# An early branch hint for TensorE's last block of instructions in a decode attention kernel

## Chip, cores, metric

The kernel runs on one core of a Trainium2 chip. The metric is the device time of one execution in microseconds (us), lower is better.

## What is computed

The reference is one decode step of grouped-query attention beside an MLP. Batch 2, one new token, model width 512, 32 query heads, 8 key/value heads, a cache of 32768 positions with head width 128, all in bfloat16. Cut to what matters:

```python
xn = layernorm(A_x)
q  = (xn @ A_wq).reshape(B, 1, 32, 128)
scores = einsum(q, repeat(k_cache, 4)) * 128 ** -0.5
o  = einsum(softmax(scores), repeat(v_cache, 4))
s  = o.reshape(B, 1, 32 * 128) @ A_wo
g  = silu(mlp_block(xn))      # with one position only w3, w4 matter
return A_x + s * g
```

The caches are 268 MB of the 280.5 MB that are read; wq, wo, w3 and w4 are the rest. With one position per sequence, the shifted halves of the MLP block are all padding, so the products with w1 and w2 contribute nothing and the kernel does not compute them.

## The kernel before

The work is cut into 16 groups, one for each pair of batch and key/value head. A group's keys are one transfer of 8 MB and its values another; the last group's are cut in halves. Both are written into fixed buffers (`kbuf`, three half-group slots that rotate; `vbuf`, two). All engines are synchronized by hand with semaphores inside one critical section: every engine has its own written order, wrapped by the small class `Queue` (waits, the instruction, an increment).

- The sync engine (SP) holds the queue of transfers: wq, w3, w4 and the first keys at the start (L310 to L313), then values and keys in turn as TensorE and ScalarE release the buffers (L448, L464, L469, L452), then wo in six parts (L477, L479; `wo_parts`, L240).
- VectorE transposes keys out of `kbuf` (L589), takes maxima, transposes the exponentials; it loops eight times over two groups each, with a branch hint of its own (L388 and L618).
- TensorE's program is written late: the prologue's products (x with wq, w3, w4) are collected in a `LateQueue` and placed at once (L685). It then waits for some constants (L686, L687), branches to the label `pe_groups` (L688), and loops 16 times over the body of one group (L689 to L734): 64 products for the scores (L698), the previous group's output (L660, L666), 64 products with the values (L722), some filling products (L673), and the closing compare-and-branch (L734). `turn` is the register that counts.
- Behind the loop stands `pe_output` (L737): the last group's output (L738 to L745), then the products on wo, part by part as they land (L746 to L773): parts for k below 5 at L760, the others at L768, between them the sum over the first (L750, which needs ScalarE's copy L646). VectorE multiplies and adds (L647, L648), and two small transfers write the result (L651).

A label with its body is a block of its own in the program; `nc.br` ends one block with a branch. The order of the instructions in memory is the order in which the blocks are written.

Of the kernel before, what the change touches and what calls it, by code (L numbers as in the profile page):

```python
# [13 lines left out]
PE = mybir.EngineType.PE  # L14
# [104 lines left out]
def kernel(  # L119
# [14 lines left out]
    nc = tc.nc  # L134
# [116 lines left out]
    def place(n):  # L251
        return n % OQ, slice(OJ - 1 - n // OQ, OJ - 1 - n // OQ + OM)

    def o_row(k, r):
        return oX[:, 1 + k:2 + k + (B - 1) * Hkv:Hkv, r]
# [47 lines left out]


    n_out = 16 * OQ
    nc.scalar.sem_inc(t_shift, n_out)
    with tc.tile_critical(sync_engine=mybir.EngineType.Pool, no_gpsimd_drain=True):
        nc.scalar.wait_ge(t_shift, n_out).then_inc(t_shift, -n_out)
# [28 lines left out]
        e_s00 = ve.op(lambda e: e.memset(sc[1][:, :], 0.0))  # L337
# [19 lines left out]
        with nc.allow_low_precision(reason="one of the terms is one, the others are zero"):  # L357
# [24 lines left out]
        e_const = ve.op(lambda v: v.tensor_copy(  # L382
            out=sel_w[:, :, :], in_=row_of[:, :].unsqueeze(1).broadcast_to([128, 4, 32])), e_row, e_ones)
# [15 lines left out]
        for i in range(NPART):  # L399
            for k in range(DK):  # L400
                for n in range(NQ):
# [5 lines left out]
                        e_xT, e_s00, inc=last)  # L407
# [13 lines left out]
        for k in range(DK):  # L421
# [7 lines left out]
        e_hf = ve.op(lambda v: v.tensor_copy(  # L429
            out=hf[:, :].rearrange("p (f b) -> p f b", b=B), in_=h4[:, :].rearrange("p (f c) -> p f c", c=32)[:, :, 0:B]), e)  # L430
# [11 lines left out]
        e_tf = ve.op(lambda v: v.tensor_add(out=t_f[:, :], in0=xn[:, :], in1=h2[0:B, :]), e_h2)  # L442
# [16 lines left out]
        e_s0 = ve.op(lambda v: v.memset(pro[:, :], 0.0))  # L459
# [21 lines left out]
        def take(eng, s, n=1):  # L481
            eng.wait_ge(s, n).then_inc(s, -n)  # L482
# [174 lines left out]
        def head_oT():  # L657
            take(nc.tensor, t_ob)
            for t in range(VT):
                ins = nc.tensor.matmul(  # L660
                    oT[:, :], lhsT=ob[:, t * Dh:(t + 1) * Dh], rhs=sel_o[:, t, :],
                    start=(t == 0), stop=(t == VT - 1))
            ins.then_inc(t_tv, 1)

        def head_xp():
            nc.tensor.matmul(  # L666
                xp_b[:, :], lhsT=sel_w[:, :, :].rearrange("p j w -> p (j w)"), rhs=on[:, :, :].rearrange("p r h -> p (r h)"),
                start=True, stop=True).then_inc(t_tv, 1)


        def fill(n):
            for _ in range(n):
                nc.tensor.matmul(pro[0:B, :], lhsT=comb[:, 0:B], rhs=ob[:, :], start=True, stop=True)  # L673

        def warm(n):
            for _ in range(n):
                nc.tensor.matmul(
                    sc[0][0:B, :], lhsT=pt[0][:, 0, 0:B], rhs=vbuf[:, 0:4 * Dh], start=True, stop=True)

        prologue, pe = pe, Queue(nc.tensor, pe.sem)  # L680
        pe.n, pe.seen = prologue.n + NG, prologue.seen
        assert prologue.n == pe_0
        turn = nc.alloc_registers("turn", engines=[PE])
        nc.regs_mov(turn, 0)
        prologue.place()  # L685
        for s, v in prologue._new((e_s00, e_const, e_hf, e_tf, e_s0)):  # L686
            nc.tensor.wait_ge(s, v)  # L687
        nc.br("pe_groups", engines=[PE])  # L688
        with nc.body("pe_groups", valid_engines=[PE]):  # L689
            for i in range(NPART):  # L690
                for r in range(NR):
# [45 lines left out]
        with nc.body("pe_output", valid_engines=[PE]):  # L737
            head_oT()  # L738
            pe.wait(e_sp, e_oX[NG - 2])
            pe.op(lambda t: t.matmul(  # L740
                wide, lhsT=sel_w[:, :, :].rearrange("p j w -> p (j w)"), rhs=oX_sp[:, :, :, :, :].rearrange("p k b j r -> p (k b j r)"),
                start=True, stop=True))
            fill(1)
            take(nc.tensor, t_vt)
            head_xp()  # L745
            for i, (a, c, r0, r1) in enumerate(wo_parts):  # L746
                if i == 3:
                    for n in range(NQ):
                        q, cols = place(n)
                        pe.op(lambda t, n=n, q=q, cols=cols: t.matmul(  # L750
                            pro[32 * q:32 * q + OM, 0:QW], lhsT=comb[:, cols], rhs=wsum[:, n * QW:(n + 1) * QW],
                            start=False, stop=False, tile_position=(0, 32 * q)), e_wsum, inc=False)
                for k in range(a, c):
                    pe.wait(e_oXz if k >= KC else e_oX[(B - 1) * Hkv + k], (d_wo[i], n_wo[i]), *((e_wide,) if i == 0 else ()))
                    for r in range(r0, r1):
                        gr = k * NQ + r
                        last = (i, k, r) == (len(wo_parts) - 1, c - 1, r1 - 1)
                        if k < KC:
                            lhs = oX_w.rearrange("p (b r) -> p b r", b=B)[:, :, gr] if i == 0 else o_row(k, r)
                            pe.op(lambda t, k=k, r=r, lhs=lhs: t.matmul(  # L760
                                qrb[32 * r:32 * r + B, :], lhsT=lhs, rhs=wo3[:, k, r * D:(r + 1) * D],
                                start=(k == 0), stop=(k == KC - 1), tile_position=(0, 32 * r)),
                                inc=(k == KC - 1 and r == NQ - 1))
                            continue
                        for n in range(NQ):
                            col = r * D + n * QW
                            q, cols = place(n)
                            pe.op(lambda t, k=k, r=r, n=n, q=q, cols=cols, col=col, last=last: t.matmul(  # L768
                                pro[32 * q:32 * q + OM, 0:QW], lhsT=oXz[:, k - KC, r, cols], rhs=wo3[:, k, col:col + QW],
                                start=(i == 2 and r == r0 and n < OQ), stop=(last and n >= NQ - OQ), tile_position=(0, 32 * q)),  # L770
                                inc=(last and n == NQ - 1))
                    if i == 2:
                        warm(1)  # L773
            nc.br("pe_done", engines=[PE])
# [37 lines left out]
```

## Time and profile before

| | |
|---|---|
| median of 3 runs | 656.04 us (655.86 to 656.45) |
| profiled execution: span, first to last instruction | 654.1 us |
| difference, what lies around the span and between executions | 1.94 us |
| PE / DVE / ACT busy | 64% / 58% / 6% |
| data queue (q1) | 280.50 MB, 99.2% of 16 DMA engines' span |
| instruction queue (q8) | 2 packets, 0.03 MB |
| mean granted TensorE clock | 0.880 |

How to read it: busy is the share of the span in which an engine executes; the DMA share is the mean over the core's 16 DMA engines, so one engine alone at work reads 0.06. Each stretch in the view by stretches has its length, the busy time of PE, PEld (weight loads), DVE, ACT and POOL with the number of instructions in brackets, the granted clock, the DMA share and GB/s. Line numbers (L698) are those of the kernel before. PEq, PEldq and DVEq rows are instructions of an engine's sequencer (branches, waits, moves).

### The profile page before, as it was taken

Reading aid. Unit: us, or ns where it says so; the run is one execution under the profiler, and the core shown is the slowest. Engines: PE = TensorE matmul, PEld = TensorE weight load, DVE = VectorE, ACT = ScalarE, POOL = GpSimd, SP = SyncE. Lnnn points to the kernel's source line nnn. Section 1 sums busy time; section 2 is a strip of 40 time slices with the busy share of each in tenths; the row PEclk is TensorE's granted clock in tenths of the full one; section 3 lists DMA queues with packets and bytes.
Section 4 is the critical chain, followed back from the end, with each engine's and each line's share of the span. In section 5 each row is a group of like instructions: output and inputs, shape, how many; then the busy total and the mean of one; then the engine's idle time right before and its main releaser. Section 6 shows DMA issues by size and latency. Waiting matters only on the chain. (4 is left out here: it accounts for less than half of the span.)

```text
span 654.1 us, 6304 instructions
## 1 busy us (share of the span) xinstructions
PE 417.4 (64%) x2476; PEld 159.3 (24%) x2476; DVE 379.4 (58%) x541; ACT 39.7 (6%) x90; POOL 10.3 (2%) x44
## 2 busy tenths in 40 slices
PE   1437386574858747485774838667484865748876
PEld 0013132221313212131321313222131322213223
DVE  5348193673919457291854729276481936738772
ACT  1200101000010100001000010100001010000101
POOL 1000000000000000000000000000000000000000
PEclk9859889697997969899796989969698896979999
DMA  8999999999999999998999999999999899999997
GB/s 367 435 449 449 442 393 449 445 449 401 437 445 449 433 405 449 445 449 389 449 445 449 417 421 445 449 445 393 449 445 449 389 449 445 449 425 411 437 429 292
DMA packets 6246, 280.54 MB, mean 429 GB/s; under 512 B 730, under 2 KB 868, under 8 KB 1380
## 3 DMA queue, kind: packets, MB, share of 16 engines
q1 hardware_dynamic: 6232, 280.50, 99.2%
q8 instruction: 2, 0.03, 0.0%
q10 hardware_dynamic: 12, 0.00, 0.0%
HBM read 280.50 MB, written 0.00 MB: 429 GB/s over the span
## 5 line engine op out<-in xcount | busy, mean ns | idle before, releaser
L589 DVE STREAM_TRANSPOSE T<-kbuf 128x1024 int32<-128x1024 int32 x256 | 294.8, 1211 | 180.1 <-DMA kbuf<-in_A_k_cache_dram 173.2
L698 PE MATMUL sc<-T,z 128*128 128x512 bf16 x1024 | 273.1, 420 | 179.5 <-PEq L482 179.2
L698 PEld LDWEIGHTS sc<-T,z 128*128 128x128 bf16 x1024 | 98.9, 104 | 346.6 <-issue 260.2
L722 PE MATMUL o<-vbuf,pt 128*16 128x512 bf16 x1024 | 70.4, 379 | 17.7 <-PEq L482 17.7
L491 ACT ACTIVATE ep<-sc,shift 128x512 bf16<-128x512 f32 x32 | 21.7, 683 | 502.7 <-ACTq L482 502.7
L722 PEld LDWEIGHTS o<-vbuf,pt 128*16 128x16 bf16 x1024 | 27.3, 88 | 64.9 <-issue 42.8
L568 DVE TENSOR_REDUCE mx<-sc 128x1 f32<-128x512 f32 x32 | 21.5, 672 | 30.1 <-PE sc L698 30.1
L673 PE MATMUL pro<-ob,comb 128*2 128x512 f32 x66 | 33.7, 592 | 0.0
L608 DVE STREAM_TRANSPOSE pt<-ep 128x512 bf16<-128x512 bf16 x32 | 22.6, 708 | 15.0 <-ACT ep L491 15.0
L710 PE MATMUL S<-mxr,same_h 128*128 128x448 f32 x32 | 15.8, 576 | 18.4 <-PEq L482 18.4
L660 PEld LDWEIGHTS oT<-sel_o,ob 128*128 128x128 f32 x136 | 17.7, 191 | 3.4 <-issue 0.7
L729 PE MATMUL S<-sm,ones_f 128*128 128x448 f32 x32 | 16.3, 592 | 0.0
L660 PE MATMUL oT<-sel_o,ob 128*128 128x4 f32 x136 | 16.2, 242 | 0.0
L600 DVE TENSOR_REDUCE shift<-S 128x1 f32<-128x64 f32 x16 | 3.6, 225 | 18.8 <-PE S L710 18.8
L496 ACT COPY ob<-o 128x512 f32<-128x512 f32 x16 | 9.4, 587 | 78.6 <-ACTq L482 78.6
L513 POOL COPY oX<-oXs 128x4 bf16 (+1 forms) x16 | 3.0, 188 | 518.7 <-POOLq L482 518.7
L710 PEld LDWEIGHTS S<-mxr,same_h 128*128 128x128 f32 x32 | 4.8, 188 | 26.1 <-issue 26.1
L572 DVE TENSOR_SCALAR mxr<-row_of,mx 128x32 f32<-128x32 f32 x32 | 7.7, 241 | 1.1
L673 PEld LDWEIGHTS pro<-ob,comb 128*2 128x2 f32 x66 | 4.2, 83 | 14.0 <-issue 10.4
L393 PE MATMUL qrb<-ident,xs_bf 34*128 34x34 bf16 x4 | 0.3, 198 | 11.1 <-DVE xs_bf L356 11.1
L729 PEld LDWEIGHTS S<-sm,ones_f 128*128 128x128 f32 x32 | 4.8, 188 | 6.9 <-issue 6.9
L506 POOL TENSOR_TENSOR z<-qr,quad 128x64 bf16<-128x64 bf16 x16 | 4.7, 294 | 103.2 <-POOLq L482 87.7
(100 smaller groups left out, 78.5 us busy)
## 6 DMA issues: line engine op xcount, KB each, us to landing
kbuf<-in_A_k_cache_dram SPq DMA_DIRECT2D x2, 4096.0 KB, 22.4
vbuf<-in_A_v_cache_dram SPq DMA_DIRECT2D x2, 4096.0 KB, 21.7
kbuf<-in_A_wq_dram SPq DMA_DIRECT2D x1, 4096.0 KB, 12.4
vbuf<-in_B_w_dram SPq DMA_DIRECT2D x2, 1792.0 KB, 18.0
kbuf<-in_A_wo_dram SPq DMA_DIRECT2D x1, 2048.0 KB, 30.8
kbuf<-in_A_wo_dram SPq DMA_DIRECT2D x3, 512.0 KB, 31.9
kbuf<-in_A_wo_dram SPq DMA_DIRECT2D x1, 384.0 KB
kbuf<-in_A_k_cache_dram SPq DMA_DIRECT2D x15, 27.5
```

What stands on the lines that cost most here:

```text
L491: nc.scalar.activation(out=ep[i][:, :], in_=sc[i][:, :], func=ACT.Exp, scale=inv_sqrt_dh, bias=shift[:, :], accum_out=rs[:, i:i + 1]).then ...
L496: nc.scalar.copy(out=ob[:, :], in_=o[:, :]).then_inc(t_ob, 1)
L568: ins = nc.vector.tensor_reduce(out=mx[:, i:i + 1], in_=sc[i][:, :], axis=AX.X, op=ALU.max)
L572: ins = nc.vector.tensor_scalar_mul(out=mxr[:, i, :], in0=row_of[:, :], scalar1=mx[:, i:i + 1]).wait_op(*c.at(t_d), "sem-ge")
L589: ins = nc.vector.transpose(out=Ts[n % T_BUFS][:, :].rearrange("p (b t k) -> p t b k", b=NB, t=RT), in_=kt[:, r * W:(r + 1) * W].rearrange ...
L608: ins = nc.vector.transpose(out=pt[h][:, :, :].rearrange("p r (t h) -> p t r h", h=rep), in_=ep[order(par).index(h)][:, :].rearrange("p (t ...
L660: ins = nc.tensor.matmul(oT[:, :], lhsT=ob[:, t * Dh:(t + 1) * Dh], rhs=sel_o[:, t, :], start=(t == 0), stop=(t == VT - 1))
L673: nc.tensor.matmul(pro[0:B, :], lhsT=comb[:, 0:B], rhs=ob[:, :], start=True, stop=True)
L698: ins = nc.tensor.matmul(sc[i][:, :], lhsT=z[:, nb, w, zc:zc + 128], rhs=Tb[:, nb, :, w], start=(r == 0 and nb == 0 and w == 0), stop=(r = ...
L710: nc.tensor.matmul(S[:, NPART * rep:NPART * (rep + SREP * 32)].rearrange("p (s c) -> p s c", s=SREP), lhsT=same_h[:, :], rhs=mxr[:, :, :]. ...
L722: ins = nc.tensor.matmul(o[32 * j:32 * j + VT * rep, :], lhsT=pt[h][:, r, a * VT * rep:(a + 1) * VT * rep], rhs=vt[:, u * VT:(u + 1) * VT, ...
L729: nc.tensor.matmul(S[:, 0:SSUM * NPART * rep].rearrange("p (s c) -> p s c", s=SSUM), lhsT=ones_f[:, :], rhs=sm[:, :, :].rearrange("p i h - ...
```

## The change

At the head of the program, ahead of the critical section, TensorE gets a marker: the place of a branch hint, an instruction that names a later branch. In place of the branch into the loop there is a block `pe_ready` with the same waits and a compare-and-branch that would go to `pe_wo` if `turn` were below zero. `turn` has just been set to zero, so it is never taken; the hint is attached to it. The other side leads over a block `pe_enter` to `pe_groups`. The products on wo get the label `pe_wo`, entered with a branch from the end of `pe_output`. Nothing else differs.

```diff
     n_out = 16 * OQ
+    hint_o = nc.tensor.mark_branch_hint_location()
     nc.scalar.sem_inc(t_shift, n_out)
     with tc.tile_critical(sync_engine=mybir.EngineType.Pool, no_gpsimd_drain=True):
...
         prologue.place()
-        for s, v in prologue._new((e_s00, e_const, e_hf, e_tf, e_s0)):
-            nc.tensor.wait_ge(s, v)
-        nc.br("pe_groups", engines=[PE])
+        nc.br("pe_ready", engines=[PE])
+        with nc.body("pe_ready", valid_engines=[PE]):
+            for s, v in prologue._new((e_s00, e_const, e_hf, e_tf, e_s0)):
+                nc.tensor.wait_ge(s, v)
+            nc.tensor.br_lt(turn, 0, on_true="pe_wo", on_false="pe_enter").branch_hint(hint_o)
+        with nc.body("pe_enter", valid_engines=[PE]):
+            nc.br("pe_groups", engines=[PE])
         with nc.body("pe_groups", valid_engines=[PE]):
...
             head_xp()
+            nc.br("pe_wo", engines=[PE])
+        with nc.body("pe_wo", valid_engines=[PE]):
             for i, (a, c, r0, r1) in enumerate(wo_parts):
```

## The prediction

> **What bounds the kernel now.** I read the page's second and third parts first (busy tenths, queues), then the chain that ended last, then stretches of the tail and of the one place where the instruction queue moves anything.
>
> ```profile
> span 654.1 us, 6304 instructions
> PE 417.4 (64%) x2476; PEld 159.3 (24%) x2476; DVE 379.4 (58%) x541; ACT 39.7 (6%) x90; POOL 10.3 (2%) x44
> ...
> DMA  8999999999999999998999999999999899999997
> ...
> q1 hardware_dynamic: 6232, 280.50, 99.2%
> q8 instruction: 2, 0.03, 0.0%
> ```
>
> No compute engine is over 64% busy; the transfers take 99.2% of sixteen engines' span. The kernel is a stream of 280.5 MB that hardly pauses. The line for this change is the last: two packets of instructions, 0.03 MB together, about 16 KB each. The chain of waits says where the end is set:
>
> ```profile
> 617.12 33.53 DMA kbuf<-in_A_wo_dram
> 650.64 0.04 issue
> 650.69 0.64 PE pro L768 x16
> ```
>
> The last part of wo lands, the last products on it follow at once. So the landing of the last transfer moves the end one for one. The next view, busy time by stretch, shows the start and the tail (DMA share is the next to last column):
>
> ```profile
> 0.00:1.90 1.90, 0.00 (x0) 0.00 (x0) 0.71 (x3) 0.25 (x1) 0.96 (x7) 1.00 0.00 0
> 1.90:4.00 2.10, 0.00 (x0) 0.00 (x0) 1.25 (x3) 1.03 (x1) 1.65 (x6) 1.00 1.13 344
> 649.00:649.66 0.66, 0.66 (x19) 0.43 (x11) 0.00 (x0) 0.00 (x0) 0.00 (x0) 1.00 0.69 238
> 649.70:650.70 1.00, 0.67 (x20) 0.44 (x20) 0.00 (x0) 0.00 (x0) 0.00 (x0) 1.00 0.06 24
> ```
>
> From 649.70 to 650.70 the share is 0.06, one part in sixteen: fifteen DMA engines are done at about 649.66 and a single one works on alone for 1.0 us. Where did that engine lose its microsecond? Two stretches of the DMA view, around 71.8 us and around 649.5 us, hold the two instruction packets:
>
> ```profile
> q1 hardware_dynamic: 14, 0.92, 179.0%
> q8 instruction: 1, 0.02, 4.8%
> ```
>
> This is 71.6 to 72.8: 4.8% of sixteen engines for 1.2 us is 0.92 us of one engine. The other is in 649.4 to 650.6:
>
> ```profile
> q1 hardware_dynamic: 32, 0.04, 9.1%
> q8 instruction: 1, 0.02, 5.0%
> ```
>
> Now the first transpose of each K group on VectorE, whose wait ends with the landing of that K (four timelines):
>
> ```profile
> 41.14 1.25 DVE L589 STREAM_TRANSPOSE T<-kbuf 128x1024 int32<-128x1024 int32 x1 [10.51 <-DMA kbuf<-in_A_k_cache_dram]
> ...
> 80.93 1.25 DVE L589 STREAM_TRANSPOSE T<-kbuf 128x1024 int32<-128x1024 int32 x1 [12.71 <-DMA kbuf<-in_A_k_cache_dram]
> ...
> 119.55 1.25 DVE L589 STREAM_TRANSPOSE T<-kbuf 128x1024 int32<-128x1024 int32 x1 [11.21 <-DMA kbuf<-in_A_k_cache_dram]
> ...
> 158.14 1.25 DVE L589 STREAM_TRANSPOSE T<-kbuf 128x1024 int32<-128x1024 int32 x1 [11.47 <-DMA kbuf<-in_A_k_cache_dram]
> ```
>
> The steps are 39.79, 38.62 and 38.59 us. The step that contains 71.8 us is 1.18 us longer, and no later step is shorter by it: a load is complete when its slowest engine is, that engine fell behind once, and the queue is never empty so that it could catch up. 1.18 us there and 1.0 us alone at the tail are the same loss. The second packet, at 649.5, costs the end nothing that I can see: the share after 649.70 is that of one engine, which streams data.
>
> **The change, part by part.** These are the rows of the branches and waits on TensorE's sequencer, of the one hint that the kernel has already (on VectorE), and of the tail.
>
> ```profile
> L688 PEldq COMPARE_BRANCH  x1: 168/168/168, 30.7 to 30.7; - x1
> ...
> L734 PEldq COMPARE_BRANCH  x16: 76/208/228, 70.6 to 641.8; - x16
> ...
> L388 DVEq BRANCH_PREFETCH_HINT  x1: 56/56/56, 12.6 to 12.6; - x1
> ...
> L684 PEldq MOVE  x1: 29/29/29, 1.1 to 1.1; - x1
> ...
> L482 PEldq EVENT_SEMAPHORE  x226: 51/51/51, 43.6 to 645.7; - x113
> ...
> 11.13 0.32 PE L393 MATMUL qrb<-ident,xs_bf 34*128 34x34 bf16 x4 [11.13 <-DVE xs_bf L356]
> ...
> 43.66 1.86 PE L698 MATMUL sc<-T,z 128*128 128x512 bf16 x4 [16.24 <-PEq L482]
> ...
> 645.86 0.38 DVE L634 TENSOR_REDUCE T<-T 128x32 bf16<-128x128 f32 x1
> 646.29 0.10 PEld L666 LDWEIGHTS xp<-on,sel_w 128*128 128x128 bf16 x1 [0.86 <-issue]
> 646.30 0.18 PE L666 MATMUL xp<-on,sel_w 128*128 128x16 bf16 x1
> 646.41 0.53 PEld L760 LDWEIGHTS qrb<-kbuf,T 128*2 128x2 bf16 x16
> ...
> 647.74 0.59 ACT L646 COPY T<-qrb 128x512 f32<-128x512 f32 x1 [3.57 <-PE qrb L760]
> 648.59 0.46 PEld L768 LDWEIGHTS pro<-kbuf,oXz 128*4 128x4 bf16 x16 [1.21 <-issue]
> ...
> 649.07 0.81 PE L750 MATMUL pro<-T,comb 128*4 128x128 f32 x8
> ```
>
> *The instructions.* One hint on TensorE's sequencer at about 1.1 us, where the MOVE stands: on VectorE it took 56 ns; TensorE's first work is ten microseconds later. Three more branches at most where L688 stands (into the ready block, the never-taken one, out of it): 3 x 168 to 228 ns, 0.5 to 0.7 us, between 30.8 us and the first product of the loop at 43.66, which waits for the K data; nothing. If that cover were gone they would cost 0.7 us once. One branch into the products on wo, behind the xp product: 168 to 228 ns on the sequencer, which has passed its wait before xp at 645.7 and must next wait for L634 of VectorE, done at 646.24. So the branch is over by 645.95, 0.29 us early. Were it late by its whole length, L760 would start 0.2 us later and the products on the landed parts after 648.59 would still wait for their landings. Zero. The loop itself gains no instruction.
>
> *The fetch.* The packet at 71.8 follows TensorE's first back edge (70.6, 0.21 us long) by about a microsecond and comes once. I read it as TensorE's code behind the loop, loaded at first need; the products on wo are that code. TensorE has the longest program, so it is the likeliest owner, but no row names one. A hint at 1.1 us that names the block of the wo products asks for those 16 KB before the stream. Taking the packet out of 71.8 is worth between 1.00 us (the tail) and 1.18 us (the K step): the engine that lagged is level again. TensorE would follow: L750 needs the copy L646, done at 648.33, so it runs from 648.4 to 649.2; the parts behind it land by 649.66 and still end last.
>
> But the 16 KB have to be moved some time. DMA share is 0.00 up to 1.9 us and full afterwards. If the packet runs within the 0.8 us left before 1.9, it costs nearly nothing, and the gain is 1.0 to 1.18. If it gets in behind the first data packets it takes 0.92 us from one engine exactly as at 71.8, the lag is there from the first microseconds on, and the gain is 0 (bound from below a loss of 0.2, should it fall on an engine that starts late). At 71.8 about a microsecond passed between the branch and the packet; from 1.1 us that points to 2.1, just inside the stream. I take the middle, 0.5 us, because the first data packets do not all start at once and part of it can fall in the gap.
>
> *Sum.* Span 654.1 - 0.5 = 653.6. The median of 656.04 stands 1.94 above this span (what lies around it, and other executions), so 653.6 + 1.94 = 655.5.
>
> [...]
>
> **The rivals.**
>
> *Nothing moves (24%).* The hint names code that is in the store already, or the packet at 71.8 is not what it names, and both packets stay. For it: VectorE's own hint at 12.6 us left no instruction packet near 12.6 us. Against: its target, a short loop, need not have been missing. Time: 656.0.
>
> *The fetch is paid again (26%); this ends slower.* The place is the one engine with TensorE's instruction packets. The hint brings in one line early, in the stream; the packet at 71.8 comes all the same since it is the line after, or the line that TensorE wanted next was put aside for the hinted one and is fetched when the never-taken branch falls through at 30.7 us. TensorE's 12.8 us of waiting there hide the stall; the engine's lag they do not hide. Each further packet adds 0.92 to 1.18 us: one (12%) gives 657.0 to 657.2, two (half of the rest) 657.9 to 658.4, three about 659. It decides from the second extra packet on, or from one with the runs' spread on top. For it: at 71.8 a packet came although the code it brought was not needed for 570 us, so the fetcher works ahead by its own order. Against: only two packets in the whole run.
>
> *The loop loses its line (6%).* The hinted line takes the place of one that the loop uses and each pass fetches it again: 16 x 0.92 to 1.18 = 14.7 to 18.9 us, 671 to 675. The quoted back edges and the missing packets speak against it.
>
> **How the numbers follow.** Forecast 44%, own range 654.9 to 656.1 (gain 1.18 to loss 0.1). About 0.2%, 1.3 us, is what a measurement of this kernel can tell from no change. A gain of 1.18 with the runs' spread (655.86 to 656.45, 0.3 to either side) can read as more: 10 of the 44. Slower by over 0.2%: half of the 12 for one extra packet, the 14 for more, the 6 of the loop, 26 in all. Within: 34 + 24 + 6 = 64. The range goes from 654.7, the best end with a little spread, to 658.4, two extra packets; left out are the loop (6), three packets (7) and some 3 at the lower end.
>
> **What would show it.** Right: the first part's q8 packet stands in the first 5 us and none near 71.8; the steps between first K transposes are all near 38.6; the stretch of DMA share 0.06 at the tail is shorter than 1.0 us. Nothing moved: the 39.8 step and the packet at 71.8 are there. Paid again: three or more q8 packets, the tail stretch 2 us or longer. Wrong altogether: a tail in which the products on wo wait for TensorE's sequencer and not for a landing, or L734's branches far over 208 ns.

## The result, and the profile after

The change made the kernel slower: 660.40 us median (656.02 to 662.36, 20 executions) against 656.03 us (655.73 to 656.45, 20 executions) before, a ratio of 1.0057 with a 95% interval of 1.0042 to 1.0072. The forecast was 655.5 us in a range of 654.7 to 658.4; the time lies above it. The 20 executions do not agree as those of the kernel before do: four lie at 656.0 to 656.3, two at 658.4 to 658.7, fourteen at 659.5 to 662.4. The profiled one took 659.53 us, 1.8 us more than its span.

The page of the kernel after, the same lines as before the change:

```profile
span 657.7 us, 6273 instructions
PE 415.5 (63%) x2444; PEld 161.6 (25%) x2476; DVE 379.9 (58%) x541; ACT 39.7 (6%) x90; POOL 10.3 (2%) x44
...
q1 hardware_dynamic: 6232, 280.50, 98.9%
q8 instruction: 3, 0.05, 0.0%
```

The work is the same. The span is 3.6 us longer, the transfers' share has gone from 99.2% to 98.9%, and there is one packet of instructions more. The chain of waits ends as before: the last of wo lands, 0.04 us of issue, the last products. So the end is still set by the stream, and the question is where the stream lost 3.6 us. Two stretches of the DMA view, 0 to 10 us and 50 to 60 us, give the packets' places; the stretch from 60 to 80 us, where one stood before the change, has none:

```profile
q8 instruction: 1, 0.02, 0.8%
...
q8 instruction: 1, 0.02, 0.6%
```

The records put them at 2.07 and 55.21 us (the third is at the tail, 652.83). The first is the one that the hint asks for, close to where the prediction expected it. The second was not expected. What TensorE does at that time is in its timeline from 43 to 62 us (start, length, instructions, and in brackets the idle time before them with what ended it), first of the kernel before, then of the kernel after:

```profile
43.66 9.19 PE L698 MATMUL sc<-T,z 128*128 128x512 bf16 x32 [16.24 <-PEq L482]
```

```profile
44.48 7.19 PE L703 MATMUL sc<-T,z 128*128 128x512 bf16 x23 [14.85 <-PEq L483]
57.39 3.57 PE L703 MATMUL sc<-T,z 128*128 128x512 bf16 x8 [5.71 <-issue]
```

Before, the first 32 score products of the loop's first pass run without a break. After, TensorE stops behind 24 of them, at 51.7 us, and stands for 5.71 us (23 have a record; the weight loads show that the first one's is missing). "issue" means that it waits for nothing that the profile shows. VectorE is not what it waits for, since VectorE itself stands for TensorE at that time:

```profile
59.29 1.25 DVE L590 STREAM_TRANSPOSE T<-kbuf 128x1024 int32<-128x1024 int32 x1 [5.67 <-PE sc L703]
```

I read the stop as a wait for instructions that are not there: the packet at 55.21 us falls into that time, and the products go on 2.2 us later. No row says what the packet holds.

TensorE is not the bound, so why does it cost anything? Because of what hangs on the 29th of these products: the code gives the increment on which SP's request for the second keys waits (`if i == 0 and r == NR - 1 and nb == 0 and w == 0: ins.then_inc(pe.sem, 1)`, r being 7 there, four products to each r). SP's timelines, before and after:

```profile
52.20 0.35 SPq L464 DMA_DIRECT2D kbuf<-in_A_k_cache_dram  x1
...
72.27 0.33 SPq L448 DMA_DIRECT2D vbuf<-in_A_v_cache_dram  x1
```

```profile
59.71 0.36 SPq L465 DMA_DIRECT2D kbuf<-in_A_k_cache_dram  x1
...
80.22 0.33 SPq L449 DMA_DIRECT2D vbuf<-in_A_v_cache_dram  x1
```

The second keys are asked for 7.5 us later, the second values, which wait for the end of that pass, 8.0 us later. The 7.5 us are more than the stop: the first keys land 0.4 us later, and the products behind the stop run slower (the stretch from 57 to 65 us has a granted clock of 0.50, where it was 1.00 before). Everything asked for earlier is done at about 60 us, so the stream runs dry: counted from the packets' records and averaged over the 16 engines, 1.0 us at 59 to 61 us and 0.6 us at 80 to 82 us, none before the change. The coarser view by stretches, before and then after, has it in the DMA share (the column before the last) over the same 84 us:

```profile
41.00:125.00 84.00, 53.20 (x297) 20.14 (x298) 50.64 (x65) 4.07 (x10) 0.96 (x4) 0.85 1.00 431
```

```profile
41.00:125.00 84.00, 52.97 (x286) 21.07 (x292) 48.30 (x63) 4.06 (x10) 0.96 (x4) 0.83 0.97 413
```

0.03 of 84 us would be 2.5 us; two rounded digits don't say it closer. How late the loads come is read from VectorE's first transpose of each K group (four timelines, after):

```profile
41.58 1.25 DVE L590 STREAM_TRANSPOSE T<-kbuf 128x1024 int32<-128x1024 int32 x1 [8.73 <-DMA kbuf<-in_A_k_cache_dram]
...
82.83 1.25 DVE L590 STREAM_TRANSPOSE T<-kbuf 128x1024 int32<-128x1024 int32 x1 [6.65 <-DMA kbuf<-in_A_k_cache_dram]
...
122.36 1.25 DVE L590 STREAM_TRANSPOSE T<-kbuf 128x1024 int32<-128x1024 int32 x1 [12.64 <-DMA kbuf<-in_A_k_cache_dram]
...
161.16 1.25 DVE L590 STREAM_TRANSPOSE T<-kbuf 128x1024 int32<-128x1024 int32 x1 [11.10 <-DMA kbuf<-in_A_k_cache_dram]
```

The steps are 41.25, 39.53 and 38.80 us, against 39.79, 38.62 and 38.59 before: 1.46, 0.91 and 0.21 us more. With a start that is 0.44 us later (the packet at 2.07 us) the fourth landing is 3.02 us late, most of the span's 3.6; by the eighth it is 3.61 us, though the packets' records show no further dry stretch.

### The profile page after: what moved, and what is told of

Its sections match the earlier page's. It is cut to its first block, busy times and chain, and to the rows that moved or that the text cites. A ratio compares the mean times of both kernels' runs of the same rounds, so it can differ in the third digit from the quotient of the medians.

```text
span 657.7 us, 6273 instructions
## 1 busy us (share of the span) xinstructions
PE 415.5 (63%) x2444; PEld 161.6 (25%) x2476; DVE 379.9 (58%) x541; ACT 39.7 (6%) x90; POOL 10.3 (2%) x44
## 3 DMA queue, kind: packets, MB, share of 16 engines
q1 hardware_dynamic: 6232, 280.50, 98.9%
## 5 line engine op out<-in xcount | busy, mean ns | idle before, releaser
L703 PE MATMUL sc<-T,z 128*128 128x512 bf16 x992 | 268.6, 422 | 184.5 <-PEq L483 177.3
## 6 DMA issues: line engine op xcount, KB each, us to landing
kbuf<-in_A_wq_dram SPq DMA_DIRECT2D x1, 4096.0 KB, 12.9
```

The lines of the kernel that those rows point to most:

```text
L703: ins = nc.tensor.matmul(sc[i][:, :], lhsT=z[:, nb, w, zc:zc + 128], rhs=Tb[:, nb, :, w], start=(r == 0 and nb == 0 and w == 0), stop=(r = ...
```

## The experiments

Theory A: the early load of the hinted code leaves code missing that the loop's first pass needs; TensorE stands in front of the products that release the K buffer, the second keys are asked for too late, and the stream runs dry. Rivals: the new labels and branches cost something; the fetches cost it by their lag alone; the stop itself, or the lower clock behind it, costs it elsewhere. The expectations number variants of A, and each says what its variant gives there; a "line" in them, as in the prediction's rivals, is the code that one packet of 16 KB is taken to bring.

**The labels without the hint.** The kernel after, without the marker and the attachment; the blocks and the never-taken branch stay.

```diff
-    hint_o = nc.tensor.mark_branch_hint_location()
...
-            nc.tensor.br_lt(turn, 0, on_true="pe_wo", on_false="pe_enter").branch_hint(hint_o)
+            nc.tensor.br_lt(turn, 0, on_true="pe_wo", on_false="pe_enter")
```

> The changed kernel without its hint: the labels, the never-taken branch and the block of the wo products stay. Theory A (the early hinted load leaves the code of the loop's first pass missing; TensorE stalls 5.7 us at 51.7 us, the second K load is asked for at 59.7 instead of 52.2 us, and the stream runs dry): 656.0 us as before, K asked for at about 52.2 us, two instruction packets, at about 72 and 649.5 us, no idle stretch of TensorE near 51.7. Theory B (the labels and the extra branch do the harm, by shifting the code or by a branch that goes against its hint): about 660 us, with the stall at 51.7 still there.

Measured: 655.82 us (655.68 to 656.11), ratio to before 0.9997, interval 0.9987 to 1.0006. Its TensorE and SP timelines:

```profile
44.01 8.48 PE L702 MATMUL sc<-T,z 128*128 128x512 bf16 x31 [14.35 <-PEq L482]
```

```profile
51.84 0.36 SPq L464 DMA_DIRECT2D kbuf<-in_A_k_cache_dram  x1
```

No stop, an early request, two packets (71.97 and 649.15 us) as before. Labels and branches cost nothing that shows; the hint alone costs the 4.4 us.

**A late first pass without any hint.** If the late request is the price, a kernel that has no hint and starts its first pass late must pay as well. In the kernel before, TensorE waits ahead of the loop for six chained fills on GpSimd, which start once the first keys have landed.

```diff
+    t_late = sem("t_late")
...
+        po.wait(e_g)
+        nc.gpsimd.wait_ge(t_k[0], 16)
+        for j in range(6):
+            ins = nc.gpsimd.memset(shared[:, 0:2, :], 0.0)
+            if j:
+                ins.wait_op(t_late, j, "sem-ge")
+            ins.then_inc(t_late, 1)
...
+        nc.tensor.wait_ge(t_late, 6)
         nc.br("pe_groups", engines=[PE])
```

> The kernel before, without any hint, in which TensorE's first pass waits for GpSimd until about 53.5 us instead of 43.7, so that K is asked for at about 59 to 61 us instead of 52.2. It measures what a late first pass costs by itself. Theory A: 3 to 6 us more, 659 to 662, and the stream has gaps at about 60 and 80 us as in the changed kernel. Rival (the stream has enough in its queue to bear 7 us, and the loss has another cause): 656.0 us within 0.5.

Measured: 661.11 us (660.98 to 661.58), ratio 1.0080, interval 1.0063 to 1.0097.

```profile
53.09 6.93 PE L707 MATMUL sc<-T,z 128*128 128x512 bf16 x23 [23.69 <-PEq L483]
```

```profile
61.53 0.36 SPq L465 DMA_DIRECT2D kbuf<-in_A_k_cache_dram  x1
...
81.36 0.33 SPq L449 DMA_DIRECT2D vbuf<-in_A_v_cache_dram  x1
```

Two packets, no hint, no stop inside the pass beyond 0.20 us, and 5.1 us lost. A late request is enough to cost what the change costs. The same with four fills in place of six asks how much of the lateness is free:

> The kernel before, no hint, with TensorE's first pass held back by GpSimd until about 49.5 us (before 43.7, and 53.5 in the run that lost 5 us). The second K load should be asked for at about 57 us. Theory A (the loss is the time for which the stream is empty, and the values in the queue last until about 59.5 us, less some 1.5 us from the request to the first bytes): the request comes just in time or up to 0.5 us late; 656.0 to 656.6 us. Rival (every microsecond of delay in the first pass is paid): about 658 to 659 us.

Measured: 657.79 us (657.1 to 658.67) beside 656.23 us of the kernel before in that comparison, ratio 1.0024, interval 1.0014 to 1.0033. The first pass starts at 49.24 us.

```profile
58.18 0.36 SPq L465 DMA_DIRECT2D kbuf<-in_A_k_cache_dram  x1
```

I had expected 656.0 to 656.6, and that was wrong; so was, if narrowly, the rival's 658 to 659. In the profiled execution, 658.02 us, a request that comes 6.0 us later than in the kernel before loses 1.8 us. If each further microsecond is lost whole, 4.2 us were free; six fills give 4.3, 9.3 us later and 5.0 us lost in the profiled execution. The rest of the 7.5 to 8 us up to the dry stretch is not free. Part of it is the lead of a request: I had put 1.5 us from the request to the first bytes, an estimate; counted from the packets' records, the stream thins at 59.7 us and is full again at 60.6, 2.4 us behind the request (in the kernel after, 1.4 us: 59.71 to 61.1). What takes the remainder was not shown.

**The stop with a full queue.** The opposite test: let TensorE stand, and give the stream something to do. SP gets one transfer more, 2 MB from memory to memory that nothing reads, behind the first values and ahead of the second keys. It goes into the kernel after and, as the measure, into the kernel before.

```diff
         load_v(0, e_h2)
+        sp.op(lambda e: e.dma_start(out=spare, in_=row_view(A_k_cache, *groups[1])[:, 0:8192]), inc=(d_sp, 16))
         pe_0, ac_0 = pe.n, ac.n
```

> The changed kernel with one more transfer of 2 MB in SP's order, behind the first values and ahead of the second keys: from memory to memory, read by nobody. It has no other use than to keep the queue filled while TensorE stands still. Theory A1 (the loss is the emptied queue, nothing else): TensorE still idles 5 to 7 us in its first pass and the second keys are still asked for at 59 to 62 us, but the extra transfer is under way then, so the queue does not run empty; the time is that of e14 plus 0 to 1.2 us (one instruction packet more), and the executions no longer scatter over 6 us. Rival A4 (the stall itself, the lowered clock or the packets delay something else): e14 plus 3.5 to 6 us, as without the cover.

> The kernel before with the same extra transfer of 2 MB. Both theories: no stall, and the time is longer by the transfer alone: 2 MB at the 436 GB/s of the stretch 45 to 105 us is 4.8 us if only the reading counts, up to 9.6 us if the writing takes as much again, so 660.8 to 665.6 us. This is the measure for e13.

Measured: after with the cover 662.42 us (661.68 to 663.06), before with the cover 662.35 us (661.71 to 662.91). The cover costs 6.35 us, and the change on top of it 0.07 us, well inside the executions' spread (1.2 to 1.4 us, four executions each). TensorE, SP and the stretch of the kernel after with the cover, and that stretch of its measure:

```profile
44.79 7.48 PE L706 MATMUL sc<-T,z 128*128 128x512 bf16 x23 [14.56 <-PEq L486]
59.61 3.52 PE L706 MATMUL sc<-T,z 128*128 128x512 bf16 x8 [7.35 <-issue]
```

```profile
61.94 0.36 SPq L468 DMA_DIRECT2D kbuf<-in_A_k_cache_dram  x1
...
81.45 0.33 SPq L451 DMA_DIRECT2D vbuf<-in_A_v_cache_dram  x1
```

```profile
41.00:125.00 84.00, 51.26 (x286) 19.84 (x290) 45.43 (x60) 4.07 (x10) 0.96 (x4) 0.87 0.99 422
```

```profile
41.00:125.00 84.00, 48.80 (x286) 19.03 (x290) 45.03 (x60) 4.06 (x10) 0.96 (x4) 0.87 1.00 424
```

The stop is there, and longer than in the kernel after (7.35 against 5.71 us); the request comes at 61.94 us, later than in any profile of the kernel after; and nothing is lost that the executions could tell: the DMA share is 0.99 beside 1.00, and the packets' records show no dry stretch in either kernel. The executions scatter no more than those of the measure. So the loss is the emptied queue: not the stop as such, not the clock, and not the packets, of which this kernel has three (2.05, 57.3 and 655.21 us) against two in its measure (71.5 and 655.57 us). Its last part of wo even lands at 657.33 us, that of the measure at 657.65.

**The place of the hint.** Three kernels move the marker only: behind the whole prologue, behind its first four transposes, and behind 37 of its instructions, the product for the queries being the last.

```diff
-    hint_o = nc.tensor.mark_branch_hint_location()
...
         prologue.place()
+        hint_o = nc.tensor.mark_branch_hint_location()
```

> The changed kernel with the hint moved behind the prologue's products, at about 29 us. Theory A1 (the hinted block takes the place of the line that TensorE needs next, whenever it comes): a packet at about 30 to 33 us, a second one at about 55 us, the stall of about 5 us at 51.7, 658 to 662 us. Theory A2 (only a hint in the first microsecond keeps the next line from being loaded; later that line is in the store and stays): a packet at 30 to 33 us, none at 55, no stall, 656.0 us within 0.5.

```diff
+        kept = prologue.kept
+        prologue.kept = kept[:4]
+        prologue.place()
+        hint_o = nc.tensor.mark_branch_hint_location()
+        prologue.kept = kept[4:]
         prologue.place()
```

> The changed kernel with the hint behind TensorE's first four transposes, at about 11 us; at 24.6 us it had brought no packet at all. Theory A2 (a hint is acted on only while the line behind the one in use is not loaded yet, in the first microsecond): no packet before 70 us, no stall, 656.0 us within 0.4. Theory A1 (a hint loads its block whenever it comes, and the late one was ignored for another reason): a packet at 12 to 15 us, a stall near 51 us, 658 to 662 us.

> The changed kernel with the hint behind the query products, at about 18.5 us. At 11.6 us it brought a packet and cost 5.7 us, at 24.6 us no packet and cost nothing. Theory A1: with a packet near 20 us there is the stall and 660 to 662 us, without one 656.0; the two go together in either case. Rival (the loss hangs on the time at which the hint comes and not on its load): a packet without a loss, or a loss without a packet.

 (as in the diff above, with 37 in place of 4)

| marker | hint ran at | packets at | idle in the first pass | K asked for at | time (range), ratio with interval |
|---|---|---|---|---|---|
| head of the program (after) | 0.82 | 2.07, 55.21, 652.83 | 5.71 | 59.71 | 660.40 (656.02 to 662.36), 1.0057 [1.0042, 1.0072] |
| behind four transposes | 11.58 | 15.3, 57.42, 655.1 | 6.61 | 62.11 | 661.67 (660.85 to 661.92), 1.0084 [1.0067, 1.0101] |
| behind 37 instructions | 18.54 | 23.48, 649.58 | none | 53.26 | 655.99 (655.87 to 656.55), 0.9999 [0.9989, 1.0008] |
| behind the prologue | 24.6 | 71.74, 649.23 | none | 52.29 | 656.00 (655.77 to 656.62), 1.0002 [0.9992, 1.0012] |

The hint at 11.6 us behaves as the one at the head, which A1 had said. The one at 24.6 us loads nothing: the packet stays at 71.7 us, while all variants of A had expected one at 30 to 33 us. The one at 18.5 us does what the change was thought to do: the packet has moved from 71.8 to 23.5 us, and TensorE does not stop behind it. The rows of its first stretch with a packet (18 to 28 us), of SP, and of the second and third K groups' landings:

```profile
q8 instruction: 1, 0.02, 0.6%
```

```profile
53.26 0.36 SPq L464 DMA_DIRECT2D kbuf<-in_A_k_cache_dram  x1
```

```profile
42.26 1.25 DVE L589 STREAM_TRANSPOSE T<-kbuf 128x1024 int32<-128x1024 int32 x1 [9.84 <-DMA kbuf<-in_A_k_cache_dram]
...
80.86 5.75 DVE L589 STREAM_TRANSPOSE T<-kbuf 128x1024 int32<-128x1024 int32 x5 [11.57 <-DMA kbuf<-in_A_k_cache_dram]
```

The first keys land 1.12 us later than in the kernel before, the step is 38.60 us in place of 39.79, and the second keys land where they did (80.86 against 80.93). The one engine's lag is paid at 23.5 us in place of 71.8 us, and the time is the same. So A1's sentence that the stop comes wherever the load comes is wrong as well, and the rival of that expectation fits: a load alone does not bring the stop (a packet at 23.48 us and no idle time in the first pass). That it has to come at a time at which it leaves code missing is my reading; no row shows it.

**What the hint names.** One kernel puts the hint at the head of the program on the loop's closing branch, so that it names the loop itself (the blocks of the change are left out); another lets it name the products on wo from the third part on, 41 instructions further (behind the first five k; the expectation calls that the fifth part).

```diff
-            nc.br_lt(turn, NG, on_true="pe_groups", on_false="pe_output", engines=[PE])
+            nc.tensor.br_lt(turn, NG, on_true="pe_groups", on_false="pe_output").branch_hint(hint_o)
```

> The kernel before with a hint at the same early place that names the loop's own closing branch, whose target is the head of the loop. Theory A1 (the harm is the line that the hinted load puts in place of another; the head of the loop lies in the line that is in use): no packet at 2 us, no stall, 656.0 us within 0.4. Theory A3 (any hint in the first microsecond stops the load of the next line): a packet near 55 us, a stall before the 93rd weight load, about 660 us.

```diff
-            nc.tensor.br_lt(turn, 0, on_true="pe_wo", on_false="pe_enter").branch_hint(hint_o)
+            nc.tensor.br_lt(turn, 0, on_true="pe_wo2", on_false="pe_enter").branch_hint(hint_o)
...
+            wo_products(0, 2)
+            nc.br("pe_wo2", engines=[PE])
+        with nc.body("pe_wo2", valid_engines=[PE]):
+            wo_products(2, len(wo_parts))
```

> The changed kernel with its label and hint moved 41 instructions further into the products on wo, behind the fifth part; the hint's place stays the first microsecond. Theory A1 (the line that is loaded and the line that is lost are whole blocks of code; 41 instructions do not matter unless a boundary lies between): a packet at 2 us, the stall before the 93rd weight load, 659 to 662 us. If instead no packet comes at 2 us and the time is 656.0, the target's place decides whether the hint does anything, as in the padded kernel.

The loop's name is harmless: 656.02 us (655.85 to 656.37), ratio 1.0003, interval 0.9993 to 1.0012, no packet near 2 us, no stop, keys asked for at 52.88 us. It is not without effect: the packet of 71.8 us, which came behind the first back edge (70.6 us), now comes at 110.5 us, behind the second (109.4 us). The later part of wo costs as the change does: 660.68 us (657.74 to 662.54), ratio 1.0077, interval 1.0060 to 1.0094, packets at 2.07 and 54.81 us, the stop at the same place. This profile is of its shortest execution, 657.74 us:

```profile
57.22 3.57 PE L703 MATMUL sc<-T,z 128*128 128x512 bf16 x8 [5.94 <-issue]
```

```profile
59.54 0.36 SPq L465 DMA_DIRECT2D kbuf<-in_A_k_cache_dram  x1
```

**The code shifted.** 116 waits that are already met, behind the prologue, shift the loop in TensorE's code; once with the change and once without it. (The expectation speaks of 58 waits; the kernels have 116.)

```diff
         prologue.place()
+        for _ in range(116):
+            nc.tensor.wait_ge(*e_xT)
```

> The changed kernel with 58 waits that are already met put behind the prologue, so that the loop begins just behind the place at which TensorE stalled. Theory A: the missing code is now needed at about 30 us, where TensorE has more than ten microseconds to wait for K anyhow; packets at 2 and at 30 to 35 us, no stall in the first pass, the second K load asked for at 52 to 53 us, 656.0 us within 0.7. Rival (the harm comes from what the hinted load at 2 us does to the transfers, or from the later prologue, and not from the place of the stall): 659 to 661 us all the same.

> The kernel before with the same met waits ahead of the loop, and no hint. The padded kernel with the hint had packets at 35.4 and 74.5 us and none at 2 us. If the hint did its work there, this one has other packets, and a stall in the first pass or at the output is possible: 656 to 660 us. If in that execution the hint did nothing, this one has the same two packets, at about 35 and 74 us, and 656.0 us within 0.4.

Measured: 656.02 us (655.83 to 656.19), ratio 1.0000 [0.9990, 1.0010], and 655.90 us (655.75 to 656.28), ratio 1.0000 [0.9991, 1.0010]. The first looked as theory A had it, but the second takes the point away: both have their packets at 35.4 and 74 us (74.5 and 74.2) and none else, so with the shifted code the hint, which ran at 0.82 us, loaded nothing at all. So in this pair the effect is gone where the code lies elsewhere, and the pair tells nothing of a hint that loads.

**The kernel after, twice again**, for the scatter.

> The changed kernel once more. Its 20 executions lay at 656.0 to 656.3 (4), 658.4 to 658.7 (2) and 659.5 to 662.4 (14). Theory A: where the profiled execution is one of the long ones, a packet stands at about 55 us, TensorE idles before its 93rd weight load, and the second K load is asked for at 58 to 61 us; where it is one at 656, there is no such packet and K is asked for at about 52 us. Rival (the scatter is the tail's or the clock's): the same packets and the same first pass in both.

> The changed kernel a third time, one look. Most likely a long execution (659 to 662): packets at 2 and 55 to 58 us and a request for K at 58 to 62 us. If it is a short one (656.0 to 656.3): no packet near 55 us, no idle stretch before the 93rd weight load, the request at about 52 us.

Eight more executions lie from 655.76 to 662.77 us with a median of 660.42, ratio 1.0056 [1.0033, 1.0078]; the single one took 659.4 us. Their two profiles have the stop at the same place, 7.08 and 5.62 us long, and the request at 61.88 and 59.56 us. Set against one another, the profiled executions without a cover line up roughly by the time of the request: 51.7 to 53.7 us, no loss; 58.18, 1.8 us; 59.5 to 59.7, 1.5 to 3.5 us; 61.5 to 62.1, 4.7 to 6.0 us. The stop's length differs from execution to execution by over a microsecond, at the point where the free part of the wait is used up; that would make the time scatter, but none of the executions at 656 was profiled.

## Why the prediction was wrong

**Right.** The stream bounds the kernel, before and after (99.2% and 98.9% of sixteen engines' span). Labels, branches and the never-taken compare cost nothing (655.82 us without the hint). The hinted packet comes just inside the stream, 2.07 us where 2.1 was worked out, and a packet that moves within the stream gains nothing, the forecast's lower bound: the hint at 18.5 us measures it (0.9999).

**The step that failed** is in the second rival: "the line that TensorE wanted next was put aside for the hinted one and is fetched when the never-taken branch falls through at 30.7 us. TensorE's 12.8 us of waiting there hide the stall; the engine's lag they do not hide." The sum of the forecast shares it: it has the early fetch cost TensorE nothing. That a line is missing behind an early load is how I read the packets, the one at 55.21 us in the stop above all; no row shows what they hold. The place was wrong: TensorE stops at about 51.7 us, inside the first pass, behind the 12.8 us of waiting, and a few products ahead of the one that releases the K buffer. And the price was wrong: I counted the lag of one DMA engine for each packet, 0.92 to 1.18 us, and no emptied stream. The runs show the reverse. With the queue covered, the stop and a third packet together add 0.07 us; without the cover, the profiled executions with a late request lose 1.5 to 6.0 us. Of that rival's two signs the three packets came, but a tail stretch of 2 us with one engine at work did not: from 653.30 to 654.30 us the share is 0.16, where one engine alone reads 0.06. I read only the waits of TensorE that lie ahead of the first pass, and never how early the second keys are asked for: 52.20 us, some 8 us before the stream runs dry without them, of which a little over 4 are free. That row was in the trace.

**The forecast's gain** of 0.5 us came from the hope that the first packet falls partly into the gap ahead of 1.9 us. It came at 2.07 us, and wq's landing took 12.9 us from its request in place of 12.4. None of the gain was there.

**The third rival**, a loss in each pass, was not seen: the stop came once, in the first pass, with its packet at 55.21 us, the back edges stay at 208 ns, and the next packet comes at 652.83 us. But what the prediction set against it, the back edges and the missing packets of the kernel before, was measured without an early load. It says nothing of the first pass behind such a load, and there the stop of 5.6 to 7.4 us came (six profiles). It looks like a wait for the packet that comes during it, though it stands at no branch but between two of the score products.

**Open.** Which rule decides what a hint loads and what is then missing: at 0.8 and 11.6 us it harms, at 18.5 it loads without harm, at 24.6 it loads nothing, and nothing at 0.8 with the code shifted. That the hinted block took the place of the missing code is argued from the packets, not shown; a second hint that would bring it back was not tried. Where all of the 3.6 us lie: 1.6 us of dry queue are counted in the records (3.1 of the 5.0 us in the kernel with the late first pass); since the covered kernel loses nothing, the rest comes with the emptied queue too, but how (the landings go on falling behind, from 3.02 us at the fourth to 3.61 at the eighth), as slow filling or as uneven engines, was not taken apart. Why a few executions stay at 656 us: a shorter stop, or none, would explain it, and no profile of one exists. Whose packet the one at 649.5 us is stays unknown.

No version ran faster than the kernel before. The best of the places tried for the hint gives the same time: with the packet at 23.5 us the first keys land 1.12 us later, with the packet at 71.8 us the second ones do by about as much.

## What to carry to other kernels

In a kernel bound by its transfers, an engine that is off the critical path has a due time: when it releases the buffer for the next request. Read that time from the queue's own timeline and set it against the end of what is already queued; the difference is the upper limit of the time for which that engine may stall for nothing. Here it was about 8 us, of which a little over 4 were free. A branch hint was not free in this program: look at the instruction queue's packets and for idle time ended by "issue" before believing that it only moves a load. A cover transfer, put into both kernels, tells quickly whether a loss is an emptied queue.

## What was not expected of the hardware

- With the transfers at full load (a DMA share of 1.00 from 45 to 57 us with the change), TensorE stands for 5.6 to 7.4 us around a packet of instructions (six profiles): the packet comes 3.4 to 5.0 us after the stop begins, the products go on 2.2 to 2.4 us after the packet.
- One packet of 16 KB delays one DMA engine by about 1 us for the rest of the stream (0.92 us of packet at 71.8 us, 1.0 us of share 0.06 at the tail); a third packet did not add a second microsecond to the end (last landing at 657.33 us with the change and the cover, at 657.65 with the cover alone).
- The same hint at four places in the prologue did three different things, and one that names the loop's head moved the later packet from behind the first back edge to behind the second (71.8 to 110.5 us).
